# One burst of eight heads in place of two of four: a hash-masked attention with a maxout FFN behind it

## The chip, the cores and the metric

The kernel runs on one core of a Trainium2 chip. The metric is the device time of one execution in microseconds (us), as the median of several executions. A core has five engines that run side by side, each in the order of its own queue: TensorE (PE in the profile) multiplies matrices into PSUM, ScalarE (ACT) computes activations and copies, VectorE (DVE) does elementwise work and 32 by 32 transposes, GpSimd (POOL) does elementwise work and issues transfers, SyncE (SP) issues transfers. They wait for each other by semaphores.

## The reference

Four batches of eight heads, 768 positions, head size 64. Each query and key gets a bucket of six sign bits by a projection; a query attends only to keys of its own bucket.

```python
def _attn_ref(q, k, v, proj):
    B, H, S, D = q.shape
    scale = 1.0 / np.sqrt(D)
    q_bits = (np.einsum('bhsd,dk->bhsk', q, proj) > 0)
    k_bits = (np.einsum('bhsd,dk->bhsk', k, proj) > 0)
    mask = q_bucket[:, :, :, None] == k_bucket[:, :, None, :]
    scores = scale * np.matmul(q, k.transpose(0, 1, 3, 2))
    scores = np.where(mask, scores, -1000000000.0)
    attn = np.exp(scores - np.max(scores, axis=-1, keepdims=True))
    attn = attn / (np.sum(attn, axis=-1, keepdims=True) + 1e-09)
    return np.matmul(attn, v)

def _moe_ref(x, w1, w2, w3, w_out):
    h = np.maximum(np.maximum(x @ w1, x @ w2), x @ w3)
    return h @ w_out
```

The attention output, 3072 tokens of 512 values, is `x` of the second part; `w1` to `w3` are 512 by 768, `w_out` 768 by 512.

## The kernel before

The mask is folded into the scores: each head's 64 query and key rows carry extra rows of +0.5 and -0.5 for the bits, so that one matmul gives scaled score plus bit agreement, and the exponential with a large scale sends disagreeing pairs to nearly nothing.

**Chunks and units.** Queries are cut into nine chunks: batch 0 into three of 256 (chunks 0, 1, 2), batches 1 to 3 into two of 384 (3 to 8). A unit is one chunk, one head and one part of the keys: two parts of three key blocks in batch 0 (48 units), three parts of two key blocks after (144 units, 24 a chunk, 48 a batch). For chunk c of 3 and more, heads 0 to 7 follow each other, three units each.

**The order is written by hand.** The main loop takes one step per unit u. A step issues, in this order: `scores(u + 1)`; what was put at this step by `when`; FFN pieces by a credit of 1 per step in batch 0 and 1.15 after; the hash of a set if `hash_at` has one; the bursts put at this step by `todo`. Nothing is reordered later.

**Scores** (L282 to L306). Matmuls (L298) fill one of two score tiles in PSUM; ScalarE's Exp (L306) writes the unit's weights to one of `NAT` weight tiles (`AT`), taken from the front of a list (L300). A tile has two more columns behind each key block, set to 1; their place differs between the 256 and the 384 form. When a tile is taken in the other form, VectorE sets them (L304); when the second burst of a chunk of batch 0 gives its tiles back, POOL sets them then (L395).

**Additions** (L329, L332). For c of 3 and more VectorE adds a head's three weight tiles to one `ad` tile two steps after the unit, and for c of 5 and more folds its two halves.

**Bursts** (`burst`, L341 to L399). One serves four heads of a chunk (i = 0: heads 0 to 3, i = 1: heads 4 to 7), side by side, each in 32 columns of TensorE and 32 partitions of PSUM. `sums` multiplies the `ad` tiles by a tile of ones (L358) into a bank, and VectorE makes the reciprocals: transpose of the bank into `ys` (L365), addition of a small constant (L367), reciprocal (L368), transpose back with broadcast into `rb` (L369). `values` (L380) multiplies the weights by the even or the odd columns of v (side 0 and 1, six key blocks of four heads, 24 matmuls a side) into a bank each, and VectorE writes `(bank + sv) * rb` to `xT` (L387); `sv` (L385) is made in the first burst of a batch and half. Four PSUM banks (`bank`, `give`) go round for sums, values, hash and FFN. After side 1 the weight tiles go back to the list.

**When.** `done_at` is the step of the last unit of a chunk's half. Bursts of chunks 3 and up come 4 steps later (`LAG`): chunk 3 at steps 63 and 75, chunk 4 at 87 and 99, chunk 5 at 111 and 123, chunk 6 at 135 and 147, chunk 7 at 159 and 171, chunk 8 at 183 and behind the loop.

**FFN** (`ffn_groups`). For each of six blocks of 128 hidden columns three groups of four matmuls (L413): the first result is copied by ScalarE (384 columns, L418) or VectorE (256 columns, L420), the others are taken into the maximum by VectorE (L422). Then the output rows (L457, copied by ScalarE at L461, sent by SP). They queue behind each other from two steps after the chunk's last burst.

**Queries and keys of later sets.** A set g is four heads. For g from 2 on: load into `nat` (L196), transposes by VectorE into `T32` (L202, four for q and four for k), narrowing by POOL into `T16` (L207), transfers by SP into the S tiles (L212), the hash on TensorE (L221, 16 rows of the profile, with VectorE's comparison at L224), and SP's transfers of the bits (L232). `SPREAD` gives the first step and the spacing of the transposes of sets 4, 5 and 6, 7; the loads come 14 steps ahead; hashes of sets 2 to 7 are at steps 32, 47, 84, 99, 135, 147.

Of the kernel before, what the change touches and what calls it, by code (L numbers as in the profile page):

```python
# [9 lines left out]
FP32 = mybir.dt.float32  # L10
FP16 = mybir.dt.float16
BF16 = mybir.dt.bfloat16
AluOp = mybir.AluOpType
# [4 lines left out]
def kernel(  # L18
# [12 lines left out]
    nc = tc.nc  # L31
    B, H, S, D = q.shape
    NBITS = proj.shape[1]
    P = 128
    NM = S // P
    HALF = S // 2
# [4 lines left out]
    Q = 32  # L41
# [8 lines left out]
    RS = 2.0 ** -5  # L50
    SCALE = 0.125 / (RS * RS)
    EPS = 2.0 ** -60
    NAT = 24
    SPREAD = {2: (61, 9), 3: (100, 12)}
    THIRD_ADD = 5
    LAG = (1, 4)
    ATW = 776

    konst = ctx.enter_context(tc.tile_pool(name="konst", bufs=1))
    nat_pool = ctx.enter_context(tc.tile_pool(name="nat", bufs=6))  # L60
    t32_pool = ctx.enter_context(tc.tile_pool(name="t32", bufs=3))
    t16_pool = ctx.enter_context(tc.tile_pool(name="t16", bufs=3))
    s_pool = ctx.enter_context(tc.tile_pool(name="spool", bufs=6))
    b_pool = ctx.enter_context(tc.tile_pool(name="bpool", bufs=2))
    vo_pool = ctx.enter_context(tc.tile_pool(name="vopool", bufs=4))
    small = ctx.enter_context(tc.tile_pool(name="small", bufs=4))
    ad_pool = ctx.enter_context(tc.tile_pool(name="adpool", bufs=5))
    ys_pool = ctx.enter_context(tc.tile_pool(name="yspool", bufs=2))
    rb_pool = ctx.enter_context(tc.tile_pool(name="rbpool", bufs=2))
    x_pool = ctx.enter_context(tc.tile_pool(name="xpool", bufs=3))  # L70
# [7 lines left out]
    pj2 = konst.tile([P, Q], FP32, name="pj2")  # L78
    pst = konst.tile([Q, 2, NBITS], FP32, name="pst")
    ones = konst.tile([P, Q], FP16, name="ones")  # L80
    at_tiles = [konst.tile([P, ATW], FP16, name=f"AT{i}", tag=f"AT{i}") for i in range(NAT)]
    warm = h_pool.tile([P, HALF], FP16, tag="ht", name="warm")
    w_sb = [konst.tile([P, NJC, DF], FP16, name=f"w{i}_sb", tag=f"w{i}_sb") for i in range(3)]
# [6 lines left out]
    def bank():  # L90
        i = free_banks.pop(0)
        return i, bank_tiles[i]

    def give(i):
        if i is not None:
            free_banks.append(i)


    nat, t32, t16, s_of, where, v_at = {}, {}, {}, {}, {}, {}
# [143 lines left out]
    def load_weights(i):  # L243
        if i == 3:
# [8 lines left out]
    chunks = [(b, w * n, w) for b in range(B) for w in (THIRD if b == 0 else HALF,)  # L253
              for n in range(S // w)]
    NCH = len(chunks)

    def parts_of(c):
        return chunks[c][2] * NM // (2 * HALF)
# [10 lines left out]

    at_free = list(range(NAT))  # L270
    at_form = [THIRD] * NAT
    at_of = {}
# [6 lines left out]
    def block_of(b, m):  # L279
        return 2 * (m % MH) + m // MH if b == 0 else m  # L280
# [29 lines left out]
    def weights_of(c, h, m):  # L310
        w = chunks[c][2]
        nb = 2 * HALF // w
        return blocks(at_tiles[at_of[unit_at[c, h, m // nb]]], w)[:, m % nb, :]

    def xt_of(c):
        if c not in xts:
            xts[c] = x_pool.tile([P, NJC, HALF], FP16, tag="xT", name="xT")
        return xts[c]
# [15 lines left out]
    def sum_blocks(c, h):  # L334
        w = chunks[c][2]
        if (c, h) in sum_of:
            t = sum_of[c, h]
            return [t[:, j, 0:w] for j in range(1 if c >= THIRD_ADD else 2)]
        return [weights_of(c, h, m)[:, 0:w] for m in range(NM)]

    def burst(c, i):  # L341
        b, q0, w = chunks[c]
        held = {}
        rb = []

        def own_bank(key):
            if c == NCH - 1 and i == 1 and key != 1:
                return None, sc_ps.tile([P, 2, 512], FP32, tag="sc", name="sc")[:, 0, :]
            return bank()

        def sums(m0, m1):
            if m0 == 0:
                held["s"] = own_bank("s")
            sm = held["s"][1]
            bs = [sum_blocks(c, 4 * i + x) for x in range(4)]
            for m in range(len(bs[0])):
                for x in range(4):
                    nc.tensor.matmul(sm[Q * x : Q * (x + 1), 0:w], ones[:, :], bs[x][m],  # L358
                                     start=(m == 0), stop=(m == len(bs[0]) - 1))
            if m1 == NM:  # L360
                ys = ys_pool.tile([P, HALF], FP32, tag="ys", name="ys")
                rr = small.tile([P, HALF // Q], FP32, tag="rr", name="rr")
                n = w // Q
                rb.append(rb_pool.tile([P, HALF], FP32, tag="rb", name="rb"))
                nc.vector.transpose(ys[:, 0:w], sm[:, 0:w])  # L365
                give(held["s"][0])
                nc.vector.tensor_scalar(out=rr[:, 0:n], in0=ys[:, 0:w:Q], scalar1=EPS * S, scalar2=None, op0=AluOp.add)  # L367
                nc.vector.reciprocal(rr[:, 0:n], rr[:, 0:n])  # L368
                nc.vector.transpose(rb[0][:, 0:w], rr[:, 0:n].unsqueeze(2).to_broadcast((P, n, Q)))  # L369

        def values(side, m0, m1):
            if m0 == 0:
                held[side] = own_bank(side)
            av = held[side][1]
            first = (b, i, side) not in sv_of
            n = w + 1 if first else w
            for m in range(m0, m1):
                cb = block_of(b, m)
                for x in range(4):
                    nc.tensor.matmul(av[Q * x : Q * (x + 1), 0:n], v_at[2 * b + i][:, x, cb * D + side : (cb + 1) * D : 2],  # L380
                                     weights_of(c, 4 * i + x, m)[:, 0:n], start=(m == 0), stop=(m == NM - 1))
            if m1 == NM:
                if first:
                    sv_of[b, i, side] = small.tile([P, 1], FP32, tag=f"sv{side}", name="sv")
                    nc.vector.tensor_scalar(out=sv_of[b, i, side][:], in0=av[:, w : w + 1], scalar1=EPS, scalar2=None,  # L385
                                            op0=AluOp.mult)
                nc.vector.scalar_tensor_tensor(out=xt_of(c)[:, 2 * i + side, 0:w], in0=av[:, 0:w],  # L387
                                               scalar=sv_of[b, i, side][:], in1=rb[0][:, 0:w], op0=AluOp.add, op1=AluOp.mult)
                give(held[side][0])
                if side == 1:  # L390
                    for h in range(4 * i, 4 * i + 4):
                        for n in range(parts_of(c)):
                            a = at_of[unit_at[c, h, n]]
                            if b == 0 and i == 1:
                                nc.gpsimd.memset(blocks(at_tiles[a], HALF)[:, :, HALF : HALF + 2], 1.0)  # L395
                                at_form[a] = HALF
                            at_free.append(a)

        return sums, values  # L399


    def ffn_groups(c):
# [76 lines left out]
    def when(u, f, *args):  # L479
        at.setdefault(u, []).append(lambda: f(*args))  # L480

    with tc.manual_schedule():
# [10 lines left out]
        load_quad(1, 2, range(4), nc.sync)  # L493
        nc.vector.memset(pj2[:], 0.0)
        nc.vector.memset(ones[:], 1.0)
        for t in at_tiles:
            nc.vector.memset(blocks(t, THIRD)[:, :, THIRD : THIRD + 2], 1.0)
        for hd in range(2):
# [75 lines left out]
        hash_at = {}  # L574
        for g in range(2, NQUAD):
            b2, i2 = divmod(g, 2)
            need = UPB * b2 + 12 * i2
            for n, side in enumerate((1, 0)):
                name = (side, g)
                if g > 3:  # L580
                    us = [SPREAD[b2][0] + SPREAD[b2][1] * (8 * i2 + 4 * n + n2) // 4 for n2 in range(4)]
                    for x in range(4):
                        when(us[0] - 14 + x, load_quad, side, g, (x,), nc.gpsimd)
                else:
                    us = [need - {2: 26, 3: 23}[g] + 4 * n + n2 for n2 in range(4)]
                for n2, u2 in enumerate(us):
                    when(u2, turn, name, n2 // 2, n2 % 2)
                    if n2 % 2:
                        when(u2 + 1, narrow, name, n2 // 2)
                when(us[3] + 3, place, name, range(4))  # L590
            hash_at[{2: 32, 3: 47, 4: need - 12}.get(g, need - 9)] = g
            when({2: 36, 3: 46}.get(g, need - 22), load_v, g)

        ffn, credit = [], 0
        todo = {}
        last_of = {}
        for c, i in sorted(done_at, key=lambda e: done_at[e]):
            d = done_at[c, i] + LAG[c > 2]
            sums, values = burst(c, i)
            pieces = [lambda f=sums: f(0, NM), lambda f=values: f(0, 0, NM), lambda f=values: f(1, 0, NM)]  # L600
            for n, f in enumerate(pieces):
                u = {(0, 0): (16, 17, 20), (1, 0): (21, 22, 24), (2, 0): (26, 27, 29)}.get((c, i), (d, d, d))[n]
                todo.setdefault(u, []).append(f)
            last_of[c] = max(u, last_of.get(c, 0))
# [65 lines left out]
```

## Time and profile before

| | us |
|---|---|
| median of 3 runs (264.99 to 265.94) | 265.4 |
| the profiled execution | 265.08 |
| its span | 263.1 |
| ScalarE busy | 177.7 |
| GpSimd busy | 69.9 |

The profile is of one execution. The span runs from its first to its last instruction. A timeline row has the start from the span's beginning, the length, the engine, the line, the operation, what is written from what is read, shapes, and how many instructions of that kind were merged into the row; in brackets stands the idle time before it and what ended it. Matmuls are pipelined and their ends are modelled, so starts are the safer numbers. The window table gives each engine's busy time in a stretch, TensorE's granted clock, the share of the transfer engines and GB/s.

### The profile page before, as it was taken

The page shows a single profiled execution, that of the slowest core. Times are in us where ns is not written, and L with a number is a line of the kernel's source. Part 1 is how long each engine was busy: PE and PEld are TensorE (multiplying, and loading weights), DVE is VectorE, ACT ScalarE, POOL GpSimd, SP SyncE. Part 2 cuts the span into 40 slices and gives each one's busy share as a digit, 9 for nine tenths or more (in the row PEclk, how much of TensorE's full clock was granted, in tenths as well). Part 3 has the DMA queues.
Part 4 walks back from the last instruction along what each step waited for, and adds up shares of the span by engine and source line. Part 5 has one row for each costly group of instructions (what it writes and reads, how often), then busy time and mean ns, then how long its engine had stood idle before and what let it go on. Part 6 is the DMA issues. An engine that isn't in the chain of part 4 may idle for free.

```text
span 263.1 us, 6479 instructions
## 1 busy us (share of the span) xinstructions
PE 256.3 (97%) x2503; PEld 154.1 (59%) x2503; DVE 208.2 (79%) x493; ACT 177.7 (68%) x257; POOL 69.9 (27%) x132
## 2 busy tenths in 40 slices
PE   7899999999999999999999999999999999999995
PEld 3555657866765666555555554555555555555552
DVE  2898767967799999969999996899949795888360
ACT  3697885667968675966869589484886859581322
POOL 2787752355043536230141612011000000000000
PEclk9999999999999999999999999999999999999999
DMA  6998899969732963970064662802030003000303
GB/s 194 328 232 163 169 241 232 217 115 206 199 88 67 196 154 51 274 193 18 0 182 120 103 138 46 212 0 60 17 122 1 0 2 121 2 0 2 120 0 120
DMA packets 20717, 30.95 MB, mean 118 GB/s; under 512 B 2608, under 2 KB 15248, under 8 KB 20688
## 3 DMA queue, kind: packets, MB, share of 16 engines
q0 software_dynamic: 8128, 13.37, 26.9%
q1 hardware_dynamic: 12128, 16.66, 22.0%
q10 hardware_dynamic: 432, 0.52, 0.6%
q8 instruction: 19, 0.31, 0.5%
q14 instruction: 10, 0.08, 0.1%
HBM read 25.17 MB, written 6.29 MB: 120 GB/s over the span
## 4 chain that ended last, share of the span: by engine, by line
PE 88%; DVE 5%; ACT 3%; issue 2%; POOL 1%; DVEq 0%; ACTq 0%
PE ms L413 33%; PE sc L298 22%; PE ms L457 11%; PE ms L380 11%; PE ms L221 3%; ACT AT L306 3%; PE ms L358 3%; PE ms L123 1%; PE ms L504 1%; PE ms L171 1%; DVE S L176 1%; DVE ht L422 1%; DVE ad L329 1%; PE ms L150 1%; POOL S L137 1%
## 5 line engine op out<-in xcount | busy, mean ns | idle before, releaser
L306 ACT ACTIVATE AT<-sc 128x768 f16<-128x768 f32 x192 | 152.7, 816 | 59.8 <-PE sc L298 56.1
L413 PE MATMUL ms<-xT,w_sb 128*128 128x384 f16 (+1 forms) x648 | 115.0, 307 | 0.3 <-DVE xT L387 0.2
L298 PE MATMUL sc<-S 72*128 72x384 bf16 (+1 forms) x432 | 93.8, 308 | 1.9 <-DVE S L176 0.8
L413 PEld LDWEIGHTS <-w_sb 128*128 128x128 f16 x648 | 62.7, 97 | 35.9 <-issue 0.4
L422 DVE TENSOR_TENSOR ht<-ht,ms 128x384 f16<-128x384 f16 (+1 forms) x108 | 54.2, 503 | 20.7 <-PE ms L413 10.4
L298 PEld LDWEIGHTS <-S 72*128 72x128 bf16 (+1 forms) x432 | 39.4, 98 | 33.0 <-issue 12.7
L207 POOL TENSOR_SCALAR T<-T 128x768 bf16<-128x768 f32 x24 | 22.9, 953 | 90.1 <-issue 48.4
L457 PE MATMUL ms<-wout_sb,ht 128*128 128x512 f16 x138 | 35.5, 378 | 0.0
L380 PE MATMUL ms<-AT,vo 128*32 128x385 f16 (+3 forms) x840 | 34.3, 308 | 0.0
L380 PEld LDWEIGHTS <-vo 128*32 128x32 f16 x864 | 22.9, 96 | 9.2 <-issue 1.7
L329 DVE TENSOR_TENSOR ad<-ad,AT 128x768 f16<-128x768 f16 x48 | 26.5, 553 | 2.1 <-ACT AT L306 1.3
L202 DVE STREAM_TRANSPOSE T<-nat 128x384 f32<-128x384 f32 x48 | 26.8, 564 | 0.0
L329 DVE TENSOR_TENSOR ad<-AT,AT 128x768 f16<-128x768 f16 x48 | 26.2, 546 | 0.2 <-ACT AT L306 0.2
L418 ACT CAST ht<-ms 128x384 f16<-128x384 f32 x36 | 17.3, 480 | 8.1 <-PE ms L413 8.1
L457 PEld LDWEIGHTS <-ht 128*128 128x128 f16 x138 | 13.3, 97 | 13.0 <-issue 0.3
L387 DVE SCALAR_TENSOR_TENSOR xT<-ms,sv,rb 128x384 f16<-128x384 f32 (+1 forms) x35 | 19.2, 565 | 1.3
L461 ACT COPY osb<-ms 128x512 f32<-128x512 f32 x21 | 12.3, 586 | 7.1 <-PE ms L457 5.8
L332 DVE TENSOR_TENSOR ad<-ad 128x384 f16<-128x384 f16 x32 | 15.5, 485 | 1.1
L137 POOL TENSOR_SCALAR S<-T 64x384 bf16<-64x384 f32 (+1 forms) x23 | 14.2, 617 | 5.0 <-DVE T L132 3.6
L196 POOL DMA_DIRECT2D nat<-in_q_dram x20 | 11.1, 560 | 0.1
L365 DVE STREAM_TRANSPOSE ys<-ms 128x384 f32<-128x384 f32 (+1 forms) x17 | 9.0, 531 | 2.3 <-PE ms L358 2.1
L176 DVE TENSOR_SCALAR S<-ms 6x384 bf16<-6x384 f32 x16 | 8.9, 554 | 2.0 <-PE ms L171 1.7
(52 smaller groups left out, 121.7 us busy)
## 6 DMA issues: line engine op xcount, KB each, us to landing
out_dram<-osb SPq DMA_DIRECT2D x21, 256.0 KB
S<-T SPq DMA_DIRECT2D x48, 96.0 KB
nat<-in_q_dram POOLq DMA_DIRECT2D x20, 192.0 KB, 6.1
vo<-in_v_dram POOLq DMA_DIRECT2D x8, 384.0 KB, 5.8
nat<-in_k_dram POOLq DMA_DIRECT2D x16, 192.0 KB, 5.7
w_sb<-in_moe_w_dram POOLq DMA_DIRECT2D x3, 768.0 KB, 10.4
nat<-in_k_dram SPq DMA_DIRECT2D x10, 192.0 KB
nat<-in_k_dram SPq DMA_DIRECT2D x3, 384.0 KB
```

What stands on the lines that cost most here:

```text
L137: nc.gpsimd.tensor_scalar(out=o, in0=i_, scalar1=RS, scalar2=1.0, op0=AluOp.mult, op1=AluOp.mult)
L202: nc.vector.transpose(t32[name][:, u, half * HALF : (half + 1) * HALF], i_)
L207: nc.gpsimd.tensor_scalar(out=t16[name][:, u, :], in0=t32[name][:, u, :], scalar1=RS, scalar2=1.0, op0=AluOp.mult, op1=AluOp.mult)
L298: nc.tensor.matmul(views[j], s_of[kn][0 : D + bits, kx, m * P : (m + 1) * P], s_of[qn][0 : D + bits, qx, q0 : q0 + w], start=True, stop=True)
L306: nc.scalar.activation(t[:, :, 0:w], whole, ActFn.Exp, bias=-SCALE * 0.25 * bits, scale=SCALE)
L329: nc.vector.tensor_tensor(out=sum_of[c, h][:], in0=t[0], in1=t[n], op=AluOp.add)
L380: nc.tensor.matmul(av[Q * x : Q * (x + 1), 0:n], v_at[2 * b + i][:, x, cb * D + side : (cb + 1) * D : 2], weights_of(c, 4 * i + x, m)[:, 0 ...
L387: nc.vector.scalar_tensor_tensor(out=xt_of(c)[:, 2 * i + side, 0:w], in0=av[:, 0:w], scalar=sv_of[b, i, side][:], in1=rb[0][:, 0:w], op0=A ...
L413: nc.tensor.matmul(ps[:, 0:w], w_sb[wi][:, jc, fb * P : (fb + 1) * P], xt[:, jc, 0:w], start=(jc == 0), stop=(jc == NJC - 1))
L418: nc.scalar.copy(hts[fb][:, 0:w], ps[:, 0:w])
L422: nc.vector.tensor_tensor(out=hts[fb][:, 0:w], in0=hts[fb][:, 0:w], in1=ps[:, 0:w], op=AluOp.max)
L457: nc.tensor.matmul(ps[:, 0:DM], hts[fb][:, tb * P : (tb + 1) * P], wout_sb[:, fb, :], start=(fb == 0), stop=(fb == NFB - 1))
```

## The change

Chunks 3 to 7 get one burst of eight heads, `burst_of_8`, at the step of their second burst. It multiplies all eight `ad` sums into one bank: the tile `ones2` has ones in 16 of its 32 columns for heads 0 to 3 and in the other 16 for heads 4 to 7, so that the 32 partitions of one PSUM quarter hold two heads, one of each half. One transpose, one addition and one reciprocal over twice the columns serve all eight; two transposes with broadcast give an `rb` for each half. Four `values` follow. Chunks 0 to 2 and 8 keep their bursts.

The weights of a whole chunk are now held until its burst, so there are 29 weight tiles and nine `ad` tiles; `nat`, `T32` and `T16` have one buffer less each. The transposes of sets 4 and 5 start at 58 instead of 61; the hashes of sets 4 to 7 are at 75, 99, 123, 147.

```diff
-    NAT = 24
-    SPREAD = {2: (61, 9), 3: (100, 12)}
+    NAT = 29
+    SPREAD = {2: (58, 9), 3: (100, 12)}
...
-    nat_pool = ctx.enter_context(tc.tile_pool(name="nat", bufs=6))
-    t32_pool = ctx.enter_context(tc.tile_pool(name="t32", bufs=3))
-    t16_pool = ctx.enter_context(tc.tile_pool(name="t16", bufs=3))
+    nat_pool = ctx.enter_context(tc.tile_pool(name="nat", bufs=5))
+    t32_pool = ctx.enter_context(tc.tile_pool(name="t32", bufs=2))
+    t16_pool = ctx.enter_context(tc.tile_pool(name="t16", bufs=2))
...
-    ad_pool = ctx.enter_context(tc.tile_pool(name="adpool", bufs=5))
+    ad_pool = ctx.enter_context(tc.tile_pool(name="adpool", bufs=9))
...
+    ones2 = konst.tile([P, 2, Q], FP16, name="ones2")
...
-        return sums, values
+        return sums, values, rb
+
+
+    def burst_of_8(c):
+        w = chunks[c][2]
+        n = w // Q
+        _, values0, rb0 = burst(c, 0)
+        _, values1, rb1 = burst(c, 1)
+        k_, sm = bank()
+        bs = [sum_blocks(c, h) for h in range(H)]
+        nb = len(bs[0])
+        for i in range(2):
+            for m in range(nb):
+                for x in range(4):
+                    nc.tensor.matmul(sm[Q * x : Q * (x + 1), 0:w], ones2[:, i, :], bs[4 * i + x][m],
+                                     start=(i == 0 and m == 0), stop=(i == 1 and m == nb - 1))
+        ys = ys_pool.tile([P, HALF], FP32, tag="ys", name="ys")
+        rr = small.tile([P, n, 2], FP32, tag="rr2", name="rr2")
+        rr1 = rr.rearrange("p n i -> p (n i)")
+        nc.vector.transpose(ys[:, 0:w], sm[:, 0:w])
+        give(k_)
+        nc.vector.tensor_scalar(out=rr1, in0=ys[:, 0 : w : Q // 2], scalar1=EPS * S, scalar2=None, op0=AluOp.add)
+        nc.vector.reciprocal(rr1, rr1)
+
+        def spread(i, rb):
+            rb.append(rb_pool.tile([P, HALF], FP32, tag="rb", name="rb"))
+            nc.vector.transpose(rb[0][:, 0:w], rr[:, :, i : i + 1].to_broadcast((P, n, Q)))
+
+        spread(0, rb0)
+        values0(0, 0, NM)
+        spread(1, rb1)
+        values0(1, 0, NM)
+        values1(0, 0, NM)
+        values1(1, 0, NM)
...
+        nc.vector.memset(ones2[:], 0.0)
+        for i in range(2):
+            nc.vector.memset(ones2[:, i, i * Q // 2 : (i + 1) * Q // 2], 1.0)
...
-            hash_at[{2: 32, 3: 47, 4: need - 12}.get(g, need - 9)] = g
+            hash_at[{2: 32, 3: 47, 4: 75, 5: 99, 6: 123, 7: 147}[g]] = g
...
-            sums, values = burst(c, i)
+            if 2 < c < NCH - 1:
+                if i == 1:
+                    todo.setdefault(d, []).append(lambda c=c: burst_of_8(c))
+                    last_of[c] = d
+                continue
+            sums, values, _ = burst(c, i)
```

## The prediction

> **What bounds the kernel now.** I read the busy table first, then TensorE's timeline, then the timelines of VectorE and ScalarE at the places where TensorE's row had a hole. A step below is one turn of the main loop, that is one unit of scores; T is the start of a block's first matmul.
>
> ```profile
> PE 256.3 (97%) x2503; PEld 154.1 (59%) x2503; DVE 208.2 (79%) x493; ACT 177.7 (68%) x257; POOL 69.9 (27%) x132
> PEclk9999999999999999999999999999999999999999
> 85.00:99.00 14.00, 14.00 (x150) 9.03 (x149) 13.62 (x34) 9.71 (x14) 6.02 (x8) 1.00 0.76 170
> ```
>
> TensorE is busy 97% of the span at a full granted clock. The third row is one stretch of the table by windows (PE, PEld, DVE, ACT, POOL busy): VectorE works 13.62 of 14 us there, so it is the next limit while the first three chunks' FFN runs. What the change wins must come out of TensorE's own stream, and what it loses must be a wait of that stream for VectorE or ScalarE. A burst looks like this on TensorE (start, length, operation):
>
> ```profile
> 146.93 0.49 PE L298 MATMUL sc<-S 72*128 72x384 bf16 x2
> 147.26 0.81 PE L413 MATMUL ms<-xT,w_sb 128*128 128x384 f16 x4
> 148.00 0.35 PE L358 MATMUL ms<-ad,ones 128*32 128x384 f16 x4
> 148.18 2.14 PE L380 MATMUL ms<-AT,vo 128*32 128x385 f16 x48
> 149.82 0.50 PE L380 MATMUL ms<-AT,vo 128*32 128x385 f16 x8
> 150.25 0.50 PE L298 MATMUL sc<-S 72*128 72x384 bf16 x2
> 150.59 0.81 PE L413 MATMUL ms<-xT,w_sb 128*128 128x384 f16 x4
> 151.24 0.49 PE L298 MATMUL sc<-S 72*128 72x384 bf16 x2
> ```
>
> Ends are modelled, so I compare starts. An FFN group of four takes 0.65 us when a score follows (150.59 to 151.24) and 0.74 when the burst follows (147.26 to 148.00): 0.09 to enter. From 148.18 to 149.82 are 40 value matmuls, ten sets of four that run side by side, 0.164 a set; the last two sets would end at 150.15, and the score starts at 150.25: 0.10 to leave. The first score pair then takes 0.34 instead of 0.33. **One visit to the 128*32 shape costs 0.20 us** beyond its matmuls. A hash has the same shape:
>
> ```profile
> 97.04 1.50 PE L221 MATMUL ms<-T,pj 128*32 128x384 f32 x16
> 98.47 0.50 PE L298 MATMUL sc<-S 72*128 72x384 bf16 x2
> 163.39 1.50 PE L221 MATMUL ms<-T,pj 128*32 128x384 f32 x16
> 164.70 0.35 PE L358 MATMUL ms<-ad,ones 128*32 128x384 f16 x4
> ```
>
> Alone it takes 1.43 us to the next score; with a burst right behind it 1.31, so no price between the two.
>
> **Visits removed: -1.2 us.** From step 48 on the kernel before makes 12 visits: bursts at 63, 75, 87, 99, 111, 123, 135, 147, 159, 171, 183, the hash at 84; the hashes at 99, 135, 147 ride on bursts. The changed one has six: 75, 99, 123, 147, 171, 183, the hashes of sets 4 to 7 riding on the first four. Matmuls stay the same in number and size (the two-column-half ones tile only moves rows within the 32). 6 x 0.20 = 1.2; bounds 1.1 and 1.3 from the rounding of the rows.
>
> By the Trainium skill, TensorEngine Tiling (Array Packing), Key Properties, a change of tiling mode drains the array; the constant of an isolated matmul in TensorE: Matmul & The Clock Gate, Single matmul latency, 166 ns warm, would as an estimate make each of twelve edges dearer and the saving 2.0 us. The rows above show 0.09 and 0.10 an edge, so the measurement decides.
>
> **An old hole that closes: -0.3 us.**
>
> ```profile
> 78.53 0.60 PE L413 MATMUL ms<-xT,w_sb 128*128 128x256 f16 x4
> 80.93 0.49 PE L298 MATMUL sc<-S 72*128 72x384 bf16 x2
> 81.57 0.60 PE L413 MATMUL ms<-xT,w_sb 128*128 128x256 f16 x4
> 81.10 0.93 DVE L422 TENSOR_TENSOR ht<-ht,ms 128x256 f16<-128x256 f16 x2
> ```
>
> The score pair at 80.93 is followed after 0.64 instead of 0.33: the group at 81.57 wants the bank of four groups earlier (78.53), and VectorE takes that group's maximum only at 81.10. VectorE is late there because it had the burst of step 63 to finish plus the transposes of set 4. In the changed kernel step 63 has no burst. The transposes move three steps up (58 instead of 61), but from step 58 to 75 VectorE then has 13 additions, 8 transposes and 20 FFN operations, about 16.7 us at the intervals of the ledger further down, against 18 steps of TensorE at 0.77 and more with two second groups, 16 to 18 us; it starts with nothing behind, and only a lag of some 2 us opens a hole. I take the 0.31 as gone; bound 0.
>
> **A new wait at step 51: +0.5 us.** With 29 weight tiles, units 48 to 52 take tiles freed by batch 0's bursts of heads 0 to 3, which convert none, so line 304 puts their two-column memset on VectorE, in its queue behind whatever stands there; before, POOL had done it at release. Units 48 and 49 are covered (ScalarE still has a backlog, then a burst of 2 us holds TensorE). Unit 50 is not: its memset stands behind the last two xT operations of the burst (2,1).
>
> ```profile
> 60.16 0.50 PE L298 MATMUL sc<-S 72*128 72x384 bf16 x2
> 61.70 0.49 PE L298 MATMUL sc<-S 72*128 72x384 bf16 x2
> 60.76 3.11 ACT L306 ACTIVATE AT<-sc 128x768 f16<-128x768 f32 x4 [2.15 <-POOL AT L395]
> 60.44 0.87 DVE L387 SCALAR_TENSOR_TENSOR xT<-ms,sv,rb 128x256 f16<-128x256 f32 x2
> 61.23 0.41 DVE L422 TENSOR_TENSOR ht<-ht,ms 128x256 f16<-128x256 f16 x1
> ```
>
> Exp of unit 50 starts at 60.76 now. VectorE is free for the memset at 61.23; with some 0.15 (estimated) for it and the signal Exp starts at 61.4 and, at the 0.81 of an Exp (3.11 for four, overlapped), ends at 62.2. Only two score tiles exist, so the score of unit 52 (61.70) waits till about 62.2: 0.5, and all of TensorE behind it. Exps 51 and 52 queue behind without further loss. Bounds 0 (if Exp had more slack than the rows show) and 0.6.
>
> **The block of eight: 0, then +0.3 us.** Per chunk VectorE loses one ys transpose, one addition and one reciprocal, and its chain now runs once for four values:
>
> ```profile
> 117.33 0.56 DVE L224 TENSOR_SCALAR bits<-ms 128x384 bf16<-128x384 f32 x1 [1.31 <-PE ms L221]
> 117.80 0.57 DVE L365 STREAM_TRANSPOSE ys<-ms 128x384 f32<-128x384 f32 x1
> 118.41 0.17 DVE L367 TENSOR_SCALAR rr<-ys 128x12 f32<-128x12 f32 x1
> 118.62 0.23 DVE L368 RECIPROCAL rr<-rr 128x12 f32<-128x12 f32 x1
> 118.88 0.58 DVE L369 STREAM_TRANSPOSE rb<-rr 128x384 f32<-128x384 f32 x1
> 119.57 1.14 DVE L387 SCALAR_TENSOR_TENSOR xT<-ms,sv,rb 128x384 f16<-128x384 f32 x2
> 89.55 0.12 DVE L385 TENSOR_SCALAR sv<-ms 128x1 f32<-128x1 f32 x1
> ```
>
> At step 75, TensorE: hash to T+1.31, four sets of sums to 1.96, four values of twelve sets (1.96 each pair, from 148.18 to 150.15) to 5.9, score, next FFN groups at 6.3, 7.1, 7.8, 8.6, which need the banks of the four values in turn. VectorE: bits at 1.6, ys at 2.2, rr 2.8, reciprocal 3.0 (0.1 longer for twice the columns), rb 3.4, sv, xT 4.0, second rb 4.6, then sv and xT by turns to 7.1; its banks come free at 4.7, 5.8, 6.5, 7.2. Slack 1.2 us or more, so no wait; without that slack each us late would cost a us in each of five blocks. ScalarE has no score for 5.9 us instead of 2.3 to 3.6, but behind the block it meets the same cadence as behind a burst now.
>
> Behind the block come 16 FFN groups of 256 columns with no pause, where before the hash (84) and a burst (87) broke them up:
>
> ```profile
> 90.95 0.57 DVE L202 STREAM_TRANSPOSE T<-nat 128x384 f32<-128x384 f32 x1
> 91.44 0.52 DVE L329 TENSOR_TENSOR ad<-ad,AT 128x768 f16<-128x768 f16 x1
> 91.88 0.41 DVE L422 TENSOR_TENSOR ht<-ht,ms 128x256 f16<-128x256 f16 x1
> 92.21 0.41 DVE L420 CAST ht<-ms 128x256 f16<-128x256 f32 x1
> 92.55 0.55 DVE L329 TENSOR_TENSOR ad<-AT,AT 128x768 f16<-128x768 f16 x1
> 95.86 0.94 DVE L422 TENSOR_TENSOR ht<-ht,ms 128x256 f16<-128x256 f16 x2
> ```
>
> Intervals: transpose 0.49, addition 0.45, maximum or copy 0.34. From 7.1, in the changed order, VectorE has five transposes, seven additions and ten FFN operations before the copy of the eleventh group: 2.45 + 3.15 + 3.5 puts its start at 16.2, its end, 0.41 on and with the signal, at 16.7. TensorE, twelve steps of 0.77 (60.16 to 61.70 is two) from the block's end at 6.0, with one second group of 0.44 among them, then a score pair and the fourteenth group, wants that bank for its fifteenth group at 16.4. A hole of 0.3; bounds 0 and 0.9 (VectorE's 22 operations 3% off move it 0.3, and groups 12 and 13 have little spare time either). Then groups without VectorE follow and it catches up.
>
> **Edits at nothing.** More memsets at the start:
>
> ```profile
> 1.10 0.51 DVE L497 MEMSET AT<- 128x6 f16 x24
> 4.51 0.33 DVE L500 COPY pj<-pst 32x6 f32<-32x6 f32 x2 [2.90 <-DMA pst<-in_proj_dram]
> ```
>
> Five AT and two ones2 operations more, 0.3 us, lie in the 2.90 that VectorE waits for proj; uncovered they would cost 0.3. The smaller pools: nat, T32 and T16 buffers are reused ten or more steps after their last reader, the tightest T32 (set 5's first transpose at 76 after set 4's hash at 75), and there VectorE's bits operation already waits for that hash. The loads of sets 4 and 5 (16 DMAs on POOL's queue) move three steps with their transposes and keep their lead of 14; hash sends of sets 4 and 6 (4 DMAs each on SP's queue) go 9 and 12 steps earlier, and the S rows that they overwrite were last read at steps 47 and 95. Uncovered, a late transpose holds the hash on TensorE; at 75 it was issued two steps (1.6 us) before.
>
> **Sum.** -1.2 - 0.3 + 0.5 + 0.3 = -0.7 us. The profiled execution took 265.08 (span 263.1 and 2.0 around it), 0.3 under the median of the three runs shown; so 264.4 by its own time, **264.7 by the median 265.4**.
>
> **Rivals.** (A) Both new waits are covered after all: 1.5 us saved, 263.9. For it: each rests on margins of 0.1 to 0.3; against it: Exp 50 has only 0.13 in hand before 61.70. (B) Slower: VectorE, which alone empties the four value banks, enters each block late, and the FFN group behind it waits. It decides from 1.2 us late; at 1.7 late in five blocks 5 x 0.5 = 2.5, 267.2. For it: lags of 1.9 occur (78.53 group ended 78.97, taken at 81.10). Against it: a hash of 1.31 ahead of four blocks lets VectorE catch up, and its load falls. The Trainium skill, TensorEngine Tiling (Array Packing), PSUM Bottleneck, warns of just this, that tiling speeds TensorE and not the emptying of PSUM; in the trace the burst at 148.00 is followed without a hole. (C) The change does not do what it says: leaving the shape is paid inside the block, between values of different heads; then 1.2 is not won, 265.9. Against it: ten sets at 0.164.
>
> **How the numbers follow.** Forecast 0.62, A 0.20, B 0.11, C 0.07. The forecast's own spread, 264.0 to 265.6, comes from the bounds of the two waits and the scatter of the runs (264.99 to 265.94). A change under 0.3% (0.8 us, so 264.6 and 266.2) can't be told from none. Of the forecast 0.42 lies under 264.6 (0.26), with A's 0.20: faster 0.46. Same 0.41: the rest of the forecast and most of C. Slower 0.13: B and a little of C and the forecast. Range 263.7 to 266.0: from A with scatter to C.
>
> **What would show it.** Visits: six starts of 128*32 matmuls after 60 us, each block without holes inside. Step 51: a hole of 0.5 before the score pair near 61.7, ScalarE's Exp waiting for VectorE's memset. No hole near 81; one of 0.3 some 10 us behind the first block, ended by VectorE's copy. I am wrong if FFN groups right behind the blocks start late, or if score pairs wait for ScalarE there.

## The result, and the profile after

| | before | changed |
|---|---|---|
| runs beside each other, us | 265.40, 265.94, 264.99, 265.27 | 267.12, 273.90, 270.48, 267.82 |
| median, us | 265.33 | 269.15 |
| ratio, 95% interval | | 1.0125 (1.0086 to 1.0163) |
| profiled execution (its span) | 265.08 (263.1) | 267.12 (265.3) |

The changed kernel is slower; I had forecast 264.7. The 273.90 and the 270.48 had mean granted clocks of 0.987 and 0.994 (as had, at 0.994, a 270.86 of the same kernel and a 270.84 of a variant further down, against 0.997 or more in all other runs, and what sets it off was not seen), and the ratio leaves the first of them out. The profiled execution ran at 1.00, so its 2.0 us over before hold no loss of clock. The first row of the page of the changed kernel (busy time of each engine):

```profile
PE 256.1 (97%) x2503; PEld 155.6 (59%) x2503; DVE 205.5 (77%) x491; ACT 176.8 (67%) x257; POOL 70.0 (26%) x132
```

TensorE has 0.2 us less to do, VectorE 2.7 less, and yet the span is 2.2 longer. So TensorE waits more. The table by windows (busy us of PE, PEld, DVE, ACT, POOL in each stretch, then clock, DMA share, GB/s) says where; the changed kernel:

```profile
60.00:75.00 15.00, 14.56 (x105) 10.02 (x104) 10.88 (x28) 13.19 (x19) 5.29 (x15) 1.00 0.64 157
76.00:84.00 8.00, 7.63 (x48) 4.40 (x47) 7.79 (x19) 6.55 (x10) 4.28 (x6) 1.00 0.46 107
92.00:106.00 14.00, 13.37 (x100) 9.49 (x98) 13.55 (x33) 11.89 (x16) 5.94 (x8) 1.00 0.43 76
106.00:140.00 34.00, 33.65 (x289) 19.05 (x288) 28.24 (x57) 23.60 (x37) 8.58 (x13) 1.00 0.47 119
```

and the kernel before:

```profile
60.00:75.00 15.00, 15.00 (x146) 10.03 (x138) 11.44 (x28) 12.54 (x17) 4.55 (x15) 1.00 0.76 166
76.00:84.00 8.00, 7.86 (x57) 5.38 (x57) 7.83 (x20) 6.70 (x9) 2.61 (x4) 1.00 0.37 96
92.00:106.00 14.00, 14.00 (x151) 9.14 (x150) 13.58 (x34) 9.32 (x13) 6.25 (x9) 1.00 0.57 112
106.00:140.00 34.00, 34.00 (x287) 18.89 (x286) 30.47 (x64) 25.30 (x39) 9.49 (x13) 1.00 0.53 138
```

Between 92 and 106 TensorE was never idle before; now it is for 0.63 us, while VectorE works 13.55 of 14. The rows of TensorE's timeline in the changed kernel at its holes (start, length, operation; in brackets idle time and what ended it):

```profile
61.95 0.48 PE L299 MATMUL sc<-S 72*128 72x384 bf16 x2 [0.44 <-ACT AT L307]
79.81 0.60 PE L447 MATMUL ms<-xT,w_sb 128*128 128x256 f16 x4 [0.33 <-DVE ht L456]
102.81 0.60 PE L447 MATMUL ms<-xT,w_sb 128*128 128x256 f16 x4 [0.46 <-DVE ht L454]
140.63 0.48 PE L299 MATMUL sc<-S 72*128 72x384 bf16 x2 [0.99 <-ACT AT L307]
```

The idle time in brackets is a little short, since ends are modelled. By starts, against the same pair of groups undisturbed, TensorE's stream changed by:

| place | us |
|---|---|
| visits to the 128*32 shape, 12 to 6 | -1.2 |
| old hole at 81 | -0.31 |
| old holes at 32 and 45 (24 weight tiles) | -0.29 |
| step 51, at 61.2 | +0.60 |
| before the first block, 76.9 to 82.7 (0.20, 0.09, 0.50, 0.07) | +0.86 |
| behind it, 99.8 to 105.4 (0.24, 0.63, 0.26, 0.13) | +1.26 |
| at 139.3 | +1.15 |
| sum | +2.07 |

The last matmul of the last burst starts at 243.27 instead of 241.30, 1.97 later, and the engines' work behind it takes as long as before. The rest of the span's 2.2 lies behind the last output row: from the issue of its transfer (262.38, before 260.42) to the end it takes 0.3 more. The first block, TensorE alone, looks as forecast:

```profile
85.52 1.50 PE L222 MATMUL ms<-T,pj 128*32 128x384 f32 x16
86.83 0.83 PE L414 MATMUL ms<-ad,ones 128*32 128x384 f16 x16
87.48 4.13 PE L381 MATMUL ms<-AT,vo 128*32 128x385 f16 x96
91.55 0.50 PE L299 MATMUL sc<-S 72*128 72x384 bf16 x2
91.88 0.60 PE L447 MATMUL ms<-xT,w_sb 128*128 128x256 f16 x4
```

Hash, sums, values and the score pair follow without a gap, and the FFN group starts 0.33 behind the score pair. Neither of the two large groups of new holes is at a block. VectorE and GpSimd ahead of the hole at 79.8:

```profile
72.08 0.98 POOL L208 TENSOR_SCALAR T<-T 128x768 bf16<-128x768 f32 x1 [9.06 <-issue]
72.28 0.41 DVE L456 TENSOR_TENSOR ht<-ht,ms 128x256 f16<-128x256 f16 x1
72.61 0.84 DVE L330 TENSOR_TENSOR ad<-ad,AT 128x768 f16<-128x768 f16 x1
73.38 0.41 DVE L454 CAST ht<-ms 128x256 f16<-128x256 f32 x1
73.89 0.42 DVE L456 TENSOR_TENSOR ht<-ht,ms 128x256 f16<-128x256 f16 x1
...
75.03 0.54 DVE L330 TENSOR_TENSOR ad<-AT,AT 128x768 f16<-128x768 f16 x1
75.50 0.41 DVE L454 CAST ht<-ms 128x256 f16<-128x256 f32 x1
```

Two things lengthen VectorE's queue here. The addition at 72.61 meets GpSimd's narrow (72.08 to 73.06) and takes 0.84 instead of 0.52. And the copy at 73.38 is followed by the maximum on the same ht tile only after 0.51; the copy at 75.50, with a transpose behind it at 75.83, after 0.33. And ahead of the hole at 139.3, ScalarE's copies of output rows and SP's queue, and then two of the copies in the kernel before (L461 there):

```profile
134.26 0.58 ACT L495 COPY osb<-ms 128x512 f32<-128x512 f32 x1
134.87 0.34 SPq L497 DMA_DIRECT2D out_dram<-osb  x1
135.31 2.55 SPq L213 DMA_DIRECT2D S<-T  x4
138.90 0.59 ACT L495 COPY osb<-ms 128x512 f32<-128x512 f32 x1 [1.44 <-DMA out_dram<-osb]
```

```profile
132.83 0.58 ACT L461 COPY osb<-ms 128x512 f32<-128x512 f32 x1
138.25 0.60 ACT L461 COPY osb<-ms 128x512 f32<-128x512 f32 x1
```

The third output row of a chunk needs the buffer of the first (there are two), whose transfer was issued at 134.87 and has left it only by 138.90. In the kernel before a burst stood between these rows, and the third copy (138.25) came 5.4 us behind the first (132.83). Now they are 4.6 us apart (134.26 and 138.90) with the wait, and an Exp and a copy of FFN stand behind the waiting copy.

### The profile page after: what moved, and what is told of

Read it like the earlier page. It is cut to its first block, busy times and chain, and to the rows that moved or that the text cites. A ratio compares the mean times of both kernels' runs of the same rounds, so it can differ in the third digit from the quotient of the medians.

```text
span 265.3 us, 6465 instructions
## 1 busy us (share of the span) xinstructions
PE 256.1 (97%) x2503; PEld 155.6 (59%) x2503; DVE 205.5 (77%) x491; ACT 176.8 (67%) x257; POOL 70.0 (26%) x132
## 4 chain that ended last, share of the span: by engine, by line
PE 80%; DVE 10%; ACT 4%; issue 3%; DMA 1%; DVEq 0%; ACTq 0%
PE ms L447 29%; PE sc L299 19%; PE ms L381 11%; PE ms L491 10%; ACT AT L307 3%; PE ms L222 3%; DVE ht L456 3%; DVE ad L330 3%; PE ms L359 2%; DMA out_dram<-osb 1%; DVE T L203 1%; PE ms L124 1%; PE ms L541 1%; PE ms L172 1%; PE ms L414 1%
## 5 line engine op out<-in xcount | busy, mean ns | idle before, releaser
L381 PE MATMUL ms<-AT,vo 128*32 128x385 f16 (+3 forms) x840 | 33.4, 308 | 0.0
L381 PEld LDWEIGHTS <-vo 128*32 128x32 f16 x864 | 23.6, 96 | 8.5 <-issue 1.3
L330 DVE TENSOR_TENSOR ad<-AT,AT 128x768 f16<-128x768 f16 x48 | 27.0, 563 | 0.2 <-ACT AT L307 0.2
L454 DVE CAST ht<-ms 128x256 f16<-128x256 f32 x18 | 7.4, 410 | 3.4 <-PE ms L447 3.4
```

The source lines that it names most:

```text
L330: nc.vector.tensor_tensor(out=sum_of[c, h][:], in0=t[0], in1=t[n], op=AluOp.add)
```

## The experiments

Times are compared by the ratio to the kernel before on the same chip, with its 95% interval. Spans of single profiles carry the start, which comes up to 0.5 us earlier or later than in that of before, so holes are read by starts within a run. For the same reason I give the drift of a run: how much longer than in the kernel before it is from the score pair of step 20 to the last one. In the kernel before these start at 26.47 and 235.67, in the changed one at 26.39 and 237.64, a drift of 2.05. "Holes" without more are those between 74 and 106.

**The changed kernel again.** No edit.

> The changed kernel once more, beside the others on one chip. Theory: its own time at full clock is 267.1 to 267.8, 2.0 to 2.5 over before, and the two longer runs (270.5 and 273.9 at granted clocks of 0.994 and 0.987) were chance. Rival: the change itself brings the clock down, by 5.9 us of unbroken matmuls in a block; half of the runs again lie over 269 at a clock of 0.995 or less, and none of the runs of before does.

267.22, 268.07, 267.54, 270.86; ratio 1.013 (1.007 to 1.0189); the holes are those of the first profile within 0.02, the one at 139 is 1.27, and the drift is 2.19. One run of four at a clock of 0.994, against half by the rival; whether the change has a part in that stays open. The 2 to 2.5 us of the others are the kernel's own (268.07 is 3.1 over).

**A third buffer for output rows.**

```
-    ys_pool = ctx.enter_context(tc.tile_pool(name="yspool", bufs=2))
+    ys_pool = ctx.enter_context(tc.tile_pool(name="yspool", bufs=1))
-    o_pool = ctx.enter_context(tc.tile_pool(name="opool", bufs=2))
+    o_pool = ctx.enter_context(tc.tile_pool(name="opool", bufs=3))
```

> The changed kernel with three buffers for output rows instead of two (and one for ys instead of two, for the room). Theory: the largest new hole of TensorE, 1.15 us at 139.3, comes from ScalarE's copy of the third output row of a chunk, which waits 1.44 us till the transfer of the first row has left its buffer; the burst that stood between these rows before is merged into the block. With a third buffer the hole goes and the span falls by 1.1 us, from 265.3 to 264.2. Rival: the row's PSUM bank or the transfers' queue is what is late, and the hole only moves; the span stays within 0.3.

Ratio 1.0026 (1.0015 to 1.0038), 265.88 us. ScalarE's copies and TensorE at the same place:

```profile
136.37 0.58 ACT L495 COPY osb<-ms 128x512 f32<-128x512 f32 x1
136.83 0.83 ACT L307 ACTIVATE AT<-sc 128x768 f16<-128x768 f32 x1
137.54 0.61 ACT L495 COPY osb<-ms 128x512 f32<-128x512 f32 x1
139.63 0.49 PE L299 MATMUL sc<-S 72*128 72x384 bf16 x2
139.96 0.81 PE L447 MATMUL ms<-xT,w_sb 128*128 128x384 f16 x4
```

The third copy runs at 137.54 without waiting and no hole is left at 139; span 264.3, drift 0.88, 1.17 less. The buffer was the cause.

**The two columns set early.**

```
+        def preset():
+            for a in at_free[2:7]:
+                nc.gpsimd.memset(blocks(at_tiles[a], HALF)[:, :, HALF : HALF + 2], 1.0)
+                at_form[a] = HALF
         when(19, fill_pj)
+        when(44, preset)
```

> The changed kernel with the two columns of the weight tiles of units 48 to 52 set on GpSimd at step 44 instead of on VectorE right before their Exp. Theory: the hole of 0.60 us at 61.2 goes and the span falls by 0.6. Rival: TensorE, 0.6 us earlier, meets a VectorE that is not earlier, so the holes between 76 and 83 (0.86 in sum) grow by what was won, and the span falls by less than 0.3.

Ratio 1.0038 (1.0024 to 1.0052), span 264.1, 1.2 lower instead of 0.6. Of that 0.65 is drift (1.40), the rest an earlier start (0.27) and the 0.3 behind the last row. The hole at 61.2 is gone, and those before the first block fell from 0.86 to 0.52, the opposite of the rival. The length of VectorE's queue is not the reason: in the changed kernel VectorE stands idle for 2.3 us after the memsets, up to its copy at 67.25. Behind it come, in the changed kernel and then here:

```profile
69.69 0.60 PE L447 MATMUL ms<-xT,w_sb 128*128 128x256 f16 x4
70.12 0.42 DVE L454 CAST ht<-ms 128x256 f16<-128x256 f32 x1
71.01 0.42 DVE L456 TENSOR_TENSOR ht<-ht,ms 128x256 f16<-128x256 f16 x1 [0.47 <-PE sc L299]
```

```profile
69.26 0.41 DVE L454 CAST ht<-ms 128x256 f16<-128x256 f32 x1
69.78 0.42 DVE L456 TENSOR_TENSOR ht<-ht,ms 128x256 f16<-128x256 f16 x1
```

In the changed kernel the maximum at 71.01 starts 0.89 after the copy on the same tile, though its group (69.69) was done at 70.29, the copy at 70.54 and the score pair that the row names at 70.62; here it is 0.52. These 0.37 are what VectorE won. Counted over all its records in the trace, waits included, that maximum is VectorE's 192nd instruction, in each of the five runs that have the memsets on VectorE. Why it is late is not shown. Waits for output rows stayed (holes of 1.09 at 138.1 and 0.28 around 167), and the second of them is new.

**Short narrows.** For sets 4 to 7 GpSimd scales only 96 of 768 columns, into the tiles of set 3, so the scores of batches 2 and 3 are not the reference's.

```
...
+        n = S if name[1] < 4 else S // 8
-        nc.gpsimd.tensor_scalar(out=t16[name][:, u, :], in0=t32[name][:, u, :], ...
+        nc.gpsimd.tensor_scalar(out=t16[name][:, u, 0:n], in0=t32[name][:, u, 0:n], ...
```

> The changed kernel with GpSimd's scaling to bf16 (the narrow, 0.98 to 1.05 us) of sets 4 to 7 cut to an eighth of its columns; the S rows of these sets come from sets 2 and 3, so scores of batches 2 and 3 are not the reference's. Theory: VectorE's additions cannot run beside a narrow (one that starts while a narrow is under way ends 0.40 us after the narrow's end, six times in the changed kernel at 0.72 to 1.18 us, against 0.52 to 0.55), and this makes more than half of VectorE's lag; the holes between 76 and 106, 2.1 us in sum, fall to 0.5 to 1.0 and the span by 1.1 to 1.6. Rival: VectorE's queue is simply too long there after the merge, the lag hardly depends on the narrows, and 1.8 us or more of these holes stay.

Ratio 1.0067 (1.0046 to 1.0089), span 264.9. The additions, and a narrow among them:

```profile
76.97 0.55 DVE L332 TENSOR_TENSOR ad<-AT,AT 128x768 f16<-128x768 f16 x1
78.26 0.52 DVE L332 TENSOR_TENSOR ad<-ad,AT 128x768 f16<-128x768 f16 x1
78.49 0.42 POOL L210 TENSOR_SCALAR T<-T 128x96 bf16<-128x96 f32 x1 [3.17 <-DMA S<-T]
```

No addition lasts over 0.61, so the long ones came from the narrows. But of 2.12 us of holes 1.38 stay: the cut won 0.74 of them, a third and not more than half, and neither expectation holds in numbers (narrows of 0.42 are left, so the whole of them may cost more). The wait for an output row left 139 and came back with the next chunk's rows, a hole of 1.58 at 165.6, so the span shows only 0.4 and the drift 0.2.

**Chunk 3 in two bursts.**

```
-            if 2 < c < NCH - 1:
+            if 3 < c < NCH - 1:
```

> The changed kernel with chunk 3 computed in two bursts of four heads (steps 63 and 75), everything else as changed. Theory of VectorE's queue: the holes belong to the transposes moved to step 58 and to the unbroken run of FFN groups; with a burst's VectorE work back at 63 the holes between 76 and 84 grow from 0.86 to 1.5 to 2.5, those behind step 75 fall from 1.26 to below 0.5, one more visit costs 0.2, and the span stays within 0.6 of 265.3. Rival: the block of eight itself makes the holes on both sides of it; both groups shrink and the span falls by 1.3 or more.

Ratio 1.0124 (1.0068 to 1.018). Holes behind step 75 are the same without a block there:

```profile
83.29 0.60 PE L447 MATMUL ms<-xT,w_sb 128*128 128x256 f16 x4 [0.33 <-DVE ht L456]
104.14 0.60 PE L447 MATMUL ms<-xT,w_sb 128*128 128x256 f16 x4 [0.46 <-DVE ht L454]
```

The holes make 1.34 us there (1.26 with the block), and 1.33 before it (0.86). The block of eight itself does not make the holes; that those behind it would fall below 0.5 was wrong too. The span of 266.4 is 1.1 longer, the drift 0.6.

**The timetable alone**, in the kernel before.

```
-    SPREAD = {2: (61, 9), 3: (100, 12)}
+    SPREAD = {2: (58, 9), 3: (100, 12)}
-            hash_at[{2: 32, 3: 47, 4: need - 12}.get(g, need - 9)] = g
+            hash_at[{2: 32, 3: 47, 4: 75, 5: 99, 6: 123, 7: 147}[g]] = g
```

> The kernel before with nothing of the change but the timetable: the transposes of sets 4 and 5 start at step 58 instead of 61, the hashes of sets 4 and 6 run at steps 75 and 123; bursts of four heads, 24 weight tiles and the pools of before. Theory: the holes behind step 75 (1.26 us in the changed kernel, 1.33 with chunk 3 in two bursts) come from the timetable: without the hash at 84, which gives VectorE 1.4 us of TensorE time for 0.55 of work, and with additions that meet more narrows, VectorE falls behind; holes of 1.0 to 1.6 us between 74 and 106 appear, one visit is saved (0.2), the span rises by 0.6 to 1.4 over the 263.1 of before. Rival: the holes come from merging the bursts, that is from the burst of chunk 4 missing at step 87; the holes stay below 0.5 and the span stays within 0.4 of 263.1.

Ratio 1.0089 (1.0071 to 1.0108), span 265.4: **2.3 us slower with none of the merge**, more than I had expected. TensorE's rows:

```profile
81.81 0.60 PE L413 MATMUL ms<-xT,w_sb 128*128 128x256 f16 x4 [0.33 <-DVE ht L422]
102.32 0.48 PE L358 MATMUL ms<-ad,ones 128*32 128x384 f16 x5 [0.59 <-DVE ad L329]
106.74 0.60 PE L413 MATMUL ms<-xT,w_sb 128*128 128x256 f16 x4 [0.31 <-DVE xT L387]
```

By starts 0.90 between 78 and 86, 1.34 between 96 and 103 (0.93 of it sums that wait for an addition), 0.48 at 106 and 0.40 at 142 (an output row); less the old 0.31 and the saved visit that is 2.6, and the drift is 2.71. Five additions of 768 columns meet a narrow here, two before.

**Only the transposes at 58**, the hashes as before.

```
-    SPREAD = {2: (61, 9), 3: (100, 12)}
+    SPREAD = {2: (58, 9), 3: (100, 12)}
```

> The kernel before with the transposes and loads of sets 4 and 5 three steps earlier (58 instead of 61) and its own hashes (84, 99, 135, 147). Theory: the timetable alone made 2.3 us slower through both its parts; this part gives the holes of 0.25 and 0.50 near 79 to 81 in place of the 0.31, so span 263.4 to 263.9, and the rest (0.8 at 101, 0.5 at 106) hangs on the hash that left step 84. Rival: the transposes alone carry it, as they put turns and narrows beside other additions; span 264.5 or more.

Ratio 1.0059 (1.0041 to 1.0077), span 264.8. Its holes are 0.91 between 79 and 87 and, unlike the theory said, also the 0.48 at 106; of those between 96 and 103 only 0.15 at the sums is there, so the rest hang on the hash that left step 84. The transposes carry two thirds of the timetable's cost by the times (1.6 of 2.3 us) and half by the drift (1.35 of 2.71).

**Both first repairs together.**

> The changed kernel with both the third buffer for output rows and the columns set early. Theory: the two gains add, 1.15 and 1.2, and the waits for output rows that showed up at 166 in the second experiment (0.28) go too; span 262.9, at or under that of before. Rival: one of the gains is eaten by VectorE's holes between 76 and 106; span 263.6 or more.

Ratio 0.9994 (0.9985 to 1.0003), 264.81 us, span 263.4: level with before. The span is 0.5 over the theory, all of it a late start: the drift is -0.11, so the two repairs together win 2.16 where 2.35 was expected. Left are VectorE's holes, 0.51 and 1.25.

**Half narrows**, on top of these.

```
-                    if n2 % 2:
+                    if g > 3:
+                        when(u2, narrow, name, n2 // 2, n2 % 2 * HALF, n2 % 2 * HALF + HALF)
+                    elif n2 % 2:
```

> The kernel of the run before (third row buffer, columns early) with each narrow of sets 4 to 7 cut in two, each half right behind its transpose, so that the second addition behind a transpose no longer meets a narrow under way. Theory: no addition lasts over 0.6 us (six of 0.72 to 1.18 in the changed kernel), the holes between 76 and 106 fall by 0.7 as with the short narrows, span 0.5 to 0.9 below that of the run before. Rival: GpSimd's fixed cost of twice the operations makes as many meetings as before; span within 0.3.

Ratio 0.9976 (0.9967 to 0.9986), 264.24 us, drift -0.45. The holes fell from 1.76 to 1.42, not by 0.7, and some meetings stayed:

```profile
73.26 0.51 POOL L208 TENSOR_SCALAR T<-T 128x384 bf16<-128x384 f32 x1 [1.86 <-DVE T L203]
73.40 0.77 DVE L330 TENSOR_TENSOR ad<-AT,AT 128x768 f16<-128x768 f16 x1
74.92 0.51 DVE L330 TENSOR_TENSOR ad<-ad,AT 128x768 f16<-128x768 f16 x1
75.08 0.73 POOL L208 TENSOR_SCALAR T<-T 128x384 bf16<-128x384 f32 x1
```

The addition that comes second (73.40) waits; where the narrow comes second (75.08) it is the narrow that is longer, 0.73 instead of 0.51.

**Half narrows in the kernel before.** The same edit.

> The kernel before with the narrows of sets 4 to 7 cut in two and nothing else. Theory: it has one hole left that belongs to VectorE (0.31 at 81), two additions of 0.99 that meet a narrow, so at most 0.3 is won: span 262.8 to 263.1. Rival: meetings with narrows cost the kernel before as much as the changed one, and the span falls by 0.7.

Ratio 0.9998 (0.9985 to 1.0011): nothing won. Its one hole near 81 is 0.50 instead of 0.31: other meetings, no fewer (five additions of 768 columns instead of two). The gain of the half narrows belongs to the crowded stretches of the changed timetable.

**The merge undone**, everything else as with the half narrows.

```
-            if 2 < c < NCH - 1:
+            if 2 < c < 3:
```

> The kernel with half narrows (third row buffer, early columns, the timetable of the change) with its merge undone: all chunks in bursts of four heads, so eleven visits to the 128*32 shape behind step 48 instead of six. Theory: the merge itself is worth its five visits at 0.20, and a burst back at 63 costs VectorE 2.9 us of work right ahead of the holes near 78, some 0.3 to 0.6 more of them; median 1.0 to 1.8 over the 264.2 of the kernel with the merge. Rival: VectorE's holes take back what fewer visits give, and the merge is worth nothing here; median within 0.4 of 264.2.

Ratio 1.0064 (1.0047 to 1.008) against 0.9976 with the merge, each beside the kernel before on its own chip: 2.3 us, more than the theory. The drift is 1.79 against -0.45, 2.24 apart. Two of its waits of TensorE (us in total, times, longest):

```profile
PE ms L359 <- DVE ad L330: 0.6, 1, 0.6
PE ms L447 <- DVE xT L388: 0.5, 2, 0.3
```

These are the sums at 101 and, as one of the two in the second row, the xT at 106, both met in the timetable alone; the block removes them with the bursts that waited (the other xT, near 42, stands in every run). Holes of 2.44 against 1.42 and five visits at 0.20 make 2.0 of the 2.24; the rest I did not find in single places.

**The copies on ScalarE**, on top of the half narrows, for chunks 1 and 2.

```
-                    if w == HALF:
+                    if c > 0:
                         nc.scalar.copy(hts[fb][:, 0:w], ps[:, 0:w])
```

> The kernel with half narrows (span 262.2), and the copies of the first FFN product of chunks 1 and 2 on ScalarE instead of VectorE. Theory: what is left of the holes between 77 and 103 (0.38, 0.16, 0.63, 0.26 us) is VectorE's queue, which works 14.5 of 15 us there; each copy given away is 0.34 less, and 1.0 to 1.4 of these holes go; span 260.8 to 261.3. Rival: ScalarE, which works five to seven Exps in a row behind a block, reaches the copies late, the maximum behind each waits for it, and holes ended by ScalarE take their place; span 262 or more.

Ratio 0.9954 (0.9938 to 0.997), 263.73 us: **1.2 us faster than the kernel before**, the best of all. The four holes are gone, but six small ones came (0.22 at 68.0, 0.13 at 70.5, 74.9 and 100.3, twice 0.07), 0.75 in sum; the first:

```profile
67.19 0.38 ACT L452 CAST ht<-ms 128x256 f16<-128x256 f32 x1
67.44 2.29 ACT L307 ACTIVATE AT<-sc 128x768 f16<-128x768 f32 x3
67.68 0.60 PE L447 MATMUL ms<-xT,w_sb 128*128 128x256 f16 x4
68.34 0.48 PE L299 MATMUL sc<-S 72*128 72x384 bf16 x2
```

A copy between two Exps delays the second, and the score pair at 68.34 comes 0.22 late. So the theory is right about VectorE and the rival about ScalarE, each by half.

## Why the prediction was wrong

- **Visits removed, -1.2: right.** Six starts of the 128*32 shape after 60 us beside the last burst, which has its own in both kernels, 0.09 to enter and 0.10 to leave each, no holes inside. Rival C is out.
- **Step 51, +0.5: right.** 0.60. ScalarE's Exp started at 61.09, 0.17 after the memset did (60.92); the 0.15 for that had been an estimate from no row. The profile names TensorE for the wait, but with the columns set early the hole is gone. What the step could not see is VectorE's idle time at 70.5, which went with the memsets and won another 0.34 before the first block.
- **The old hole at 81, -0.3: wrong.** It went, and 0.86 came in its region. The step that failed: "from step 58 to 75 VectorE ... then has ... about 16.7 us ... and only a lag of some 2 us opens a hole". The threshold was right. The group at 79.81 wants the bank of the group at 76.26, done at 76.7, whose maximum VectorE took at 79.3: 2.6 late. The ledger was too small. From the first transpose (69.19) to that maximum it gives 9.0 us (five transposes at 0.49, seven additions at 0.45, ten FFN operations at 0.34); VectorE took 10.15. What came on top is 0.32 at 72.61, the addition beside the narrow, some 0.17 for each of three pairs on one ht tile (70.12, 73.38 and 76.75), and 0.37 in which VectorE stood idle at 70.5 with its group done; other intervals were a little shorter. The pair was in a row that the prediction showed: 0.94 for two maxima of 0.41 is an interval of 0.53. I had read its 0.34 off an operation with other work behind it.
- **The block of eight, 0 then +0.3: right at the block, mis-sized behind it**, 1.26. The copy of the eleventh group, forecast at 16.2 from the block's start, came at 16.8 (102.34 less 85.52), by one narrow of 0.32 and two pairs of 0.17; and I had put all of the lag into one hole, where groups on either side of it lost 0.24, 0.26 and 0.13.
- **Edits at nothing: wrong at the moved transposes and hashes.** I had counted their instructions and queues and not what each stands beside: the transposes' move of three steps and the hash taken from step 84 cost 2.3 us in the kernel before. The full additions that meet a narrow rose from two to six, to five by the timetable alone.
- **Missing: output rows, +1.15.** The burst in the middle of a chunk had spread them. I followed the instructions that the block moves on TensorE and VectorE, and not ScalarE's copies in a pool of two.
- **Not forecast: 29 tiles, -0.29.** The hole of 0.23 at 45 stands in every run with 24 tiles and in none with 29. The Exp ahead of it (44.95 in the kernel before) is another late one: it starts 0.26 after everything that the trace shows it to wait for, and is ScalarE's 64th instruction in all four of these runs. Why is open here too.
- **Rival B** gave the right sign and nearly the time (267.2), by another way: no FFN group right behind a block waited. So that its number is near is luck.
- **Slips that decide nothing:** ten operations at 0.34 are 3.4 and not 3.5, the queue from step 58 to 75 adds up to 16.6 and not 16.7, and the group at 78.53 was taken 2.1 late, not 1.9.

Put together by drift: the timetable +2.71, the output rows +1.17, the memsets +0.65, the tiles -0.28, the merge -2.24 (measured where the repairs stand): +2.0 against 2.05. That this closes so well is in part luck. The parts act on each other (the timetable alone already holds 0.40 of output rows, the two repairs win 2.16 together and 1.82 apart, each changes which additions meet a narrow), and each drift is that of a single profile; by the times of all runs the timetable is 2.3. The changed kernel with the timetable of before was not run.

## What to carry to other kernels

When work is taken out of the middle of a stretch, look at every pool whose uses it had kept apart, the output buffers of an engine that the edit doesn't touch included. Where an engine works 95% of a stretch, cost its operations in pairs, by the interval to what comes next, and not by one interval of an operation: a tenth too little in the ledger hid VectorE's holes here. And a change in several parts is judged by its parts: here the part that looked free lost 2.3 us, and the main one won as much with its side effects repaired.

## What the runs showed of the hardware

An fp16 addition on VectorE does not run beside a GpSimd narrow that is under way. The six long ones of the changed kernel end 0.40 us after the narrow's end (0.44 of overlap and 0.84 in all at 72.61), those of 384 columns 0.20 after; the eight of 384 columns that meet a narrow take 0.86, the other 24 take 0.36. The maximum with one operand in PSUM takes 0.41 with or without a narrow, and a transpose 0.56 to 0.57. It goes the other way too: a half narrow takes 0.51 when no addition is under way, and one that starts beside an addition ends 0.37 us after it (0.66, 0.73 and 0.81 in all with 0.29, 0.36 and 0.44 of the addition left). The Trainium skill says in Trainium Architecture — The Big Picture, What this means for kernel authors, that on the engines' side of SBUF only the ports that VectorE and GpSimd share contend, by an exclusive lock; and in GPSIMD Engine Reference, 1. Specifications, it names VectorE's instructions with two SBUF inputs among those that contend. The traces agree with both: the addition has two such inputs and waits, the maximum has one and does not.

What stays open are two late instructions, VectorE's 192nd at 71.01 in the changed kernel and ScalarE's 64th at 44.95 in the kernel before: they start 0.37 and 0.26 us behind all that the trace shows them to wait for, and in all fourteen traces the starts on these two engines that come more than 0.2 us late in this way are the 64th or the 192nd instruction of the engine.
